# One decode layer with cached attention and an MLP: ten idle matrix products taken out ahead of the sixth group's values, and the second MLP product split four to ten between a partial sum and the result

## The chip, the cores and the metric

The kernel runs on one core of a Trainium2 chip. The core has a matrix engine (TensorE, "PE" in the profile, with its weight loads as "PEld"), a vector engine (VectorE, "DVE"), a scalar engine (ScalarE, "ACT"), a general engine (GpSimd, "POOL"), and a queue engine (SyncE, "SP") which here only issues transfers from the device's memory (DMA). The metric is the device time of one execution in microseconds, the median of several runs.

## The reference

Four tokens (batch 4, one position each, width 448) pass through an attention block over the last 1024 cached positions and then through an MLP; both add to the running sum `h`.

```python
def _A_ref(x, k_cache, v_cache, wq, wo):          # 16 query heads, 8 key/value heads, head width 256
    W = 1024                                      # only the last 1024 of 4096 cached positions
    q = (x @ wq).reshape(B, Sq, 16, 256).transpose(0, 2, 1, 3)
    k = repeat(k_cache[:, :, Sk - W:, :], 2, axis=1)
    v = repeat(v_cache[:, :, Sk - W:, :], 2, axis=1)
    p = softmax(einsum("bhqd,bhkd->bhqk", q, k) * 256 ** -0.5)
    return einsum("bhqk,bhkd->bhqd", p, v).transpose(0, 2, 1, 3).reshape(B, Sq, 4096) @ wo

def _B_ref(x, w1, b1, w2, b2):                    # 448 -> 1792 -> 448
    return gelu(layernorm(x) @ w1 + b1) @ w2 + b2

h = x + _A_ref(layernorm(x), k_cache, v_cache, wq, wo)
return h + _B_ref(layernorm(h), w1, b1, w2, b2)
```

Everything is float32. The data that has to be read is about 88 MB: two caches of 8 x 4 MB each (as far as they are used), and the four weight matrices.

## The kernel before

**Stages.** A "group" `g` is one of the eight key/value heads with its two query heads, for all four tokens. For each group the kernel projects the queries (`project_q`), forms scores against 1024 keys (`scores_half` twice, 512 keys each), takes the softmax (`softmax`), transposes the probabilities (`transpose_p`, tiles `ppt` to `pT`), multiplies them with the cached values (`values`, tile `po`), transposes and scales the result (`transposed_output`, tiles `o`, `pot`, `oT`) and multiplies it with its slice of the output weights (`add_output`, into `acc`). The groups overlap: while one is in its values, the next is in its scores. After the last group come two layer norms and the MLP: the first product `pu` (line 416), the Gelu (line 430), transposes into `gT` (lines 435 to 442), and the second product (lines 445 to 463) into `py`, to which line 465 adds the rest; line 466 writes it out.

**Columns of the matrix engine.** With only four tokens a product uses few of the engine's 128 columns. So the kernel places four products at a time at rows 0, 32, 64 and 96 of the output, one for each token, or one for each chunk of the contraction, or one for each quarter of the output's columns.

**The second MLP product.** The contraction over 1792 runs in 14 chunks `c` of 128. There are two ways to do a chunk:

- *Through a partial sum*: one product per chunk over all 448 output columns (line 449), placed at quadrant `c % 4` of a tile `pa`. All chunks of a quadrant add up there. ScalarE then copies `pa` to `pas` (line 453), and four products with a selection matrix (`add_quadrants`, line 255) add the four quadrants up into `py`.
- *Straight into the result*: four products per chunk, one for each quarter of the output columns (128, or 64 for the last of a chunk), each at its own quadrant of `py` (line 459). Nothing has to be added up behind it.

Before, eight chunks go the first way and six the second; `add_quadrants` stands behind the second of these six, so that they run while ScalarE copies.

**Idle products.** `keep_warm(n, tile)` issues `n` products of a zero tile (bf16, 32 columns of weights, 512 columns of data) into a scratch tile; nobody reads them. They stand at places where the matrix engine would otherwise sit idle. Line 340 issues ten of them between the transposes of group 7's probabilities (line 339) and the values of group 6 (line 342).

**What sets the order.** The order on the matrix engine is the program's own order, since that engine is scheduled by hand. Transfers are all issued by SP, in program order, into three large slots (`ring`). The last three slots, `te`, hold: the keys of group 7 (`k7`, 4096 KB); the values and output weights of group 6 (`vo[0]`, 4992 KB, in one transfer); the values of group 7 in three pieces (1024, 2048 and 1024 KB); its output weights (896 KB); the first MLP weights in two pieces (`w1`, 1792 and 1344 KB: contraction chunks 0 and 1, then 2 and 3); and the second MLP weights in three pieces (`w2`, 1792, 896 and 448 KB: chunks 0 to 7, then 8 to 11, then 12 and 13). Each product waits for the piece that it reads. The SP rows for the last slots, with what each issue waits for, are these (`DMAHW0` to `DMAHW7` are eight completion counters of transfers, taken in turn; `DMA te_815<-w` are the pieces of `w2`):

```order
L57 DMA te_813<-k 128x8192 [waits DMAHW5_49,PE_49]
L57 DMA te_814<-vo 128x9984 [waits DMAHW6_49,PE_49]
L57 DMA te_815<-vo 128x2048 [waits DMAHW7_49,PE_49]
L57 DMA te_815<-vo 128x4096
...
L57 DMA te_814<-vo 128x1792
L57 DMA te_813<-w 128x3584
L57 DMA te_813<-w 128x2688
L57 DMA te_815<-w 128x3584 [waits DMAHW0_49]
L57 DMA te_815<-w 128x1792 [waits DMAHW1_49]
L57 DMA te_815<-w 128x896 [waits DMAHW2_49]
```

The counters go round: `k7` has number 0, `vo[0]` number 1, the first piece of group 7's values number 2, and so on up to the first MLP weights with 6 and 7; the three pieces of `w2` have 0, 1 and 2 again. So the second piece of `w2` is issued when `vo[0]` has landed, and the third when the first piece of group 7's values has. (A row for a second piece of 2048 columns between those of 4096 and 1792 reads like the one above it and is left out.)

Of the kernel before, what the change touches and what calls it, by code (L numbers as in the profile page):

```python
# [35 lines left out]
def block_kernel(ctx: ExitStack, tc, rows, wq0, k0, wq1, la, lb, lc, ld, k7, vo, w1, w2, out):  # L36
# [165 lines left out]
    def transpose_p(g, p):  # L202
        for h in range(2):
            pt = ps_t.tile([P, 4, P], F32, tag="t", name=f"ppt{g}_{h}")
            for c in range(4):
                nc.tensor.transpose(pt[:, c, :], p[:, (4 * h + c) * P : (4 * h + c + 1) * P], ident)  # L206

            src = pt.rearrange("p (c i) (b q) -> p c i b q", i=2, b=B)
            for i in range(2):
                nc.vector.tensor_copy(  # L210
                    pT[g % 2][:, 2 * h : 2 * h + 2, :, i * REP : (i + 1) * REP], src[:, :, i, :, :REP]
                )
# [14 lines left out]
    def columns(t, j):  # L227
        if j < 3:
            return t[:, j * P : (j + 1) * P].rearrange("p (i c) -> p i c", i=2)
        return t[:, None, 3 * P :].to_broadcast([t.shape[0], 2, H])  # L230
# [22 lines left out]
    def add_quadrants(dst, t, start):  # L253
        for j in range(4):
            nc.tensor.matmul(dst[j * Q : (j + 1) * Q], sel, columns(t, j), start=start, stop=False)

    def po_tile(g, pool=ps_o, tag="o"):
        return pool.tile([P, 2, DH], F32, tag=tag, name=f"po{g}")
# [73 lines left out]
    warm0 = ps_o.tile([P, 512], F32, tag="o", name="warm0")  # L332

    def keep_warm(n, warm):
        for _ in range(n):
            nc.tensor.matmul(warm[:Q], idle[:, :Q], idle, start=True, stop=True)  # L336

    keep_warm(2, warm0)
    transpose_p(g + 1, p)
    keep_warm(10, warm0)  # L340
    po = po_tile(g)
    values(g, vt, po)
    po_last = po_tile(g + 1, ps_t, "t")
# [98 lines left out]
        nc.scalar.copy(gT[rows, 12:, :B], put[rows, 3].rearrange("p (j i) q -> p j i q", i=2)[:, :, i, :])  # L442
    keep_warm(1, warm)

    first = 8
    pa = ps_w.tile([P, D], F32, tag="acc", name="pa")
    for c in range(first):
        j, m = c % 4, Q if c < 4 else B
# [6 lines left out]
    for c in range(first, NFC):  # L455
        for j in range(4):
            m, n = (Q, 2) if c == first else (B, 2 if j < 3 else 1)
            w = columns(w2t[c], j) if n == 2 else w2t[c][:, None, 3 * P :]
            nc.tensor.matmul(
                py[j * Q : j * Q + m, :n, :], gT[:, c, :m], w, start=(c == first), stop=(c == NFC - 1),  # L460
            )
        if c == first + 1:
            add_quadrants(py, pas, False)
    res = once.tile([P, P], F32, tag="res", name="res")
    nc.vector.tensor_add(res, py.rearrange("p i c -> p (i c)"), hb)
# [72 lines left out]
```

## Time and profile before

| | us |
|---|---|
| median of three runs | 214.65 (214.59 to 214.75) |
| the profiled execution, its own time | 214.81 |
| span in its trace, first to last instruction | 213.0 |
| PE busy | 137.4 (64% of the span) |
| DVE busy | 38.4 (18%) |
| ACT busy | 21.2 (10%) |
| bytes read from the device's memory | 88.26 MB, 415 GB/s over the span |

The table reads as follows: the matrix engine has the most work of all engines, but a third of the span it does nothing. The transfers, which are not an engine's instructions, move 415 GB/s on average over the whole span. Where the one and where the other decides has to be read from the stages, which the prediction does.

### The profile page before, as it was taken

What the parts mean: (1) busy time and instruction counts of PE and PEld (TensorE: products, weight loads), DVE (VectorE), ACT (ScalarE), POOL (GpSimd) and SP (SyncE); (2) the same over time, 40 slices, a digit from 0 to 9 for tenths busy, and PEclk for the clock granted to TensorE, in tenths of its full rate; (3) what the DMA queues carried; (4) which work ended last, traced back from release to release, by engine and by line L of the source; (5) the groups of instructions that cost most, each with busy time, mean ns of one, the idle gap of its engine ahead of it and who ended that gap; (6) DMA issues with size and microseconds to landing.
All of it is one profiled execution on the core that took longest, in us unless ns stands there. A gap on an engine that the chain in (4) does not pass through costs nothing.

```text
span 213.0 us, 2294 instructions
## 1 busy us (share of the span) xinstructions
PE 137.4 (64%) x971; PEld 48.2 (23%) x971; DVE 38.4 (18%) x167; ACT 21.2 (10%) x52; POOL 5.6 (3%) x17
## 2 busy tenths in 40 slices
PE   0456824872970595289398198239809876998993
PEld 0322211220220221023123022113202322334432
DVE  1420320320230012012114013100301223122320
ACT  0210110120020100021003001000000302000310
POOL 6100000000000000000000000000000000000110
PEclk9999995796697579769859959955965999999999
DMA  7999899999999999999999999999999998999990
GB/s 291 433 392 502 381 486 391 447 467 409 417 453 444 417 417 477 390 465 391 458 423 444 425 456 417 429 417 465 405 410 415 430 450 380 435 414 435 420 376 34
DMA packets 3289, 88.46 MB, mean 415 GB/s; under 512 B 384, under 2 KB 512, under 8 KB 1104
## 3 DMA queue, kind: packets, MB, share of 16 engines
q1 hardware_dynamic: 3248, 88.29, 96.7%
q8 instruction: 7, 0.11, 0.2%
q10 hardware_dynamic: 32, 0.05, 0.1%
q14 instruction: 2, 0.02, 0.0%
HBM read 88.26 MB, written 0.07 MB: 415 GB/s over the span
## 4 chain that ended last, share of the span: by engine, by line
DMA 64%; PE 29%; DVE 3%; ACT 1%; issue 1%; SPq 0%; ACTq 0%; DVEq 0%
DMA ta<-la 21%; DMA td<-ld 20%; DMA tb<-lb 16%; PE s L174 8%; DMA t<-k 8%; PE po L218 8%; PE ppt L206 2%; PE pu L416 2%; PE warm L336 1%; PE acc L247 1%; PE pq L154 1%; PE pot L239 1%; PE pa L449 1%; DVE o L235 1%; DVE mx L179 1%
## 5 line engine op out<-in xcount | busy, mean ns | idle before, releaser
L179 DVE TENSOR_REDUCE mx<-s 128x1 f32<-128x512 f32 x16 | 11.1, 691 | 61.0 <-PE s L174 61.0
L174 PE MATMUL s<-ta,qT 128*32 128x512 f32 x64 | 12.2, 935 | 8.9 <-DMA ta<-la 8.9
L156 ACT COPY qs<-pq 128x512 f32<-128x512 f32 x8 | 4.7, 585 | 112.3 <-PE pq L154 112.3
L190 ACT ACTIVATE p<-s,nm 128x512 f32<-128x512 f32 x16 | 10.9, 687 | 45.9 <-DVE nm L186 45.9
L174 PE MATMUL s<-td,qT 128*32 128x512 f32 x32 | 7.3, 1061 | 12.0 <-DMA td<-ld 12.0
L235 DVE TENSOR_SCALAR o<-po,rec 128x512 f32<-128x512 f32 x8 | 6.0, 751 | 47.1 <-PE po L218 47.1
L218 PE MATMUL po<-tb,pT 128*32 128x512 f32 x32 | 7.3, 1061 | 10.4 <-DMA tb<-lb 10.4
L154 PE MATMUL pq<-tc,yT 128*32 128x512 f32 (+1 forms) x20 | 3.9, 890 | 14.8 <-DMA tc<-lc 14.8
L206 PE MATMUL ppt<-ident,p 128*128 128x128 f32 x64 | 10.5, 286 | 2.0 <-ACT p L190 1.7
L218 PE MATMUL po<-tc,pT 128*32 128x512 f32 x64 | 10.5, 815 | 0.0
L160 PE MATMUL pqt<-ident,qs 128*128 128x128 f32 x32 | 6.6, 341 | 6.0 <-ACT qs L156 6.0
L174 PE MATMUL s<-tb,qT 128*32 128x512 f32 x64 | 9.1, 717 | 0.0
L206 PEld LDWEIGHTS ppt<-ident,p 128*128 128x128 f32 x64 | 6.7, 140 | 7.1 <-ACT p L190 7.1
L218 PE MATMUL po<-te,pT 128*32 128x512 f32 x64 | 7.9, 596 | 0.1
L162 DVE TENSOR_REDUCE sm<-pqt 128x16 f32<-128x64 f32 x8 | 1.8, 224 | 33.9 <-PE pqt L160 33.9
L174 PE MATMUL s<-t,qT 128*32 128x512 f32 x32 | 6.1, 925 | 2.6 <-DMA t<-k 2.6
L218 PE MATMUL po<-td,pT 128*32 128x512 f32 x64 | 7.3, 595 | 0.0
L336 PE MATMUL warm<-idle 128*32 128x512 bf16 x25 | 7.3, 382 | 0.0
L160 PEld LDWEIGHTS pqt<-ident,qs 128*128 128x128 f32 x32 | 4.2, 169 | 12.1 <-ACT qs L156 10.3
L174 PEld LDWEIGHTS s<-ta,qT 128*32 128x32 f32 x64 | 2.9, 163 | 17.4 <-issue 14.4
L239 PE MATMUL pot<-ident,o 128*128 128x128 f32 x32 | 5.2, 287 | 2.2 <-DVE o L235 2.2
L148 POOL TENSOR_TENSOR r<-ve_r,mhalf 128x1 f32<-128x1 f32 x2 | 1.1, 542 | 192.2 <-DVE ve_r L147 192.2
(129 smaller groups left out, 113.4 us busy)
## 6 DMA issues: line engine op xcount, KB each, us to landing
tc<-lc SPq DMA_DIRECT2D x2, 7936.0 KB
td<-ld SPq DMA_DIRECT2D x2, 7936.0 KB
ta<-la SPq DMA_DIRECT2D x2, 7040.0 KB, 29.4
tb<-lb SPq DMA_DIRECT2D x2, 7040.0 KB, 34.3
te<-vo SPq DMA_DIRECT2D x1, 4992.0 KB, 27.2
t<-k SPq DMA_DIRECT2D x1, 4864.0 KB, 16.4
te<-k SPq DMA_DIRECT2D x1, 4096.0 KB, 36.9
te<-w SPq DMA_DIRECT2D x2, 1792.0 KB, 28.0
```

The costliest lines, as they stand in the source:

```text
L154: nc.tensor.matmul(pq[j * Q : (j + 1) * Q, cols], y, w, start=True, stop=True)
L156: nc.scalar.copy(qs, pq)
L160: nc.tensor.transpose(pt[:, i, :], qs[:, i * P : (i + 1) * P], ident)
L174: nc.tensor.matmul(s[b * Q : (b + 1) * Q, :], qT[g % 2][:, c, b, :], kt[:, c, b, :], start=(c == 0), stop=(c == 1),)
L179: nc.vector.reduce_max(m, s, axis=AX.X)
L190: nc.scalar.activation(p[:, h * 512 : (h + 1) * 512], halves[h], AF.Exp, bias=nm, scale=SCALE, accum_out=sums[:, h : h + 1],)
L206: nc.tensor.transpose(pt[:, c, :], p[:, (4 * h + c) * P : (4 * h + c + 1) * P], ident)
L218: nc.tensor.matmul(po[b * Q : (b + 1) * Q], pT[g % 2][:, c, b, :], vt[c][:, :, b, :], start=(c == 0), stop=(c == NKC // 2 - 1),)
L235: nc.vector.tensor_scalar_mul(o, po, rec)
L239: nc.tensor.transpose(pt[:, i, c], o[:, i, c * P : (c + 1) * P], ident)
L336: nc.tensor.matmul(warm[:Q], idle[:, :Q], idle, start=True, stop=True)
L416: nc.tensor.matmul(pu[j * Q : j * Q + m, :], zT[rows, a, :m], w, start=(a == 0), stop=(a == ND - 1),)
```

## The change

The ten idle products of line 340 are taken out, and the second MLP product is divided otherwise: four chunks go through the partial sum and ten straight into the result. `add_quadrants` now stands behind chunk 7, the fourth of the straight ones.

```diff
     keep_warm(2, warm0)
     transpose_p(g + 1, p)
-    keep_warm(10, warm0)
     po = po_tile(g)
     values(g, vt, po)
...
-    first = 8
+    first = 4
     pa = ps_w.tile([P, D], F32, tag="acc", name="pa")
     for c in range(first):
         j, m = c % 4, Q if c < 4 else B
...
-        if c == first + 1:
+        if c == 7:
             add_quadrants(py, pas, False)
```

On the matrix engine, behind the transposes of group 7's probabilities (`ppt`; `te_814` holds group 6's values, `warm_859` is the scratch tile), there stood before, with nine more pairs like the one shown:

```order
L206 MATMUL ppt_1_869<-ident,p_852 128x128 [waits Activation_49]
L206 MATMUL ppt_1_869<-ident,p_852 128x128 x3
L336 LDWEIGHTS idle
L336 MATMUL warm_859<-idle 32x512
...
L218 MATMUL po_886<-te_814,pT_113 32x512 [waits DMAHW1_49,PE_49]
L218 MATMUL po_886<-te_814,pT_113 32x512 x15
```

and now:

```order
L206 MATMUL ppt_1_869<-ident,p_852 128x128 [waits Activation_49]
L206 MATMUL ppt_1_869<-ident,p_852 128x128 x3
L218 MATMUL po_876<-te_814,pT_113 32x512 [waits DMAHW1_49,PE_49]
L218 MATMUL po_876<-te_814,pT_113 32x512 x15
L218 MATMUL po_893<-te_815,pT_114 32x512 [waits DMAHW2_49,DVE_49,PE_49]
```

The values of group 6 follow the transposes directly; they still wait for `vo[0]`, counter 1.

At the end of the matrix engine's program, in the second MLP product (`te_815` holds `w2`), there stood before:

```order
L449 MATMUL pa<-te_815,gT 32x448 [waits DMAHW0_49,DVE_49,Pool_49]
L449 MATMUL pa<-te_815,gT 32x448 x3
L449 MATMUL pa<-te_815,gT 4x448 x4
L459 MATMUL py<-te_815,gT 32x128 [waits DMAHW1_49]
L459 MATMUL py<-te_815,gT 32x128 x3
L459 MATMUL py<-te_815,gT 4x128 x3
L459 MATMUL py<-te_815,gT 4x64
L255 MATMUL py<-pas,sel 32x128 [waits Activation_49]
L255 MATMUL py<-pas,sel 32x128 x3
```

and now:

```order
L448 MATMUL pa<-te_815,gT 32x448 [waits DMAHW0_49,DVE_49,Pool_49]
L448 MATMUL pa<-te_815,gT 32x448 x3
L458 MATMUL py<-te_815,gT 32x128 x4
L458 MATMUL py<-te_815,gT 4x128 x3
L458 MATMUL py<-te_815,gT 4x64
...
L255 MATMUL py<-pas,sel 32x128 [waits Activation_49]
L255 MATMUL py<-pas,sel 32x128 x3
L458 MATMUL py<-te_815,gT 4x128 [waits DMAHW1_49]
```

Four full-width products and their weights are gone, sixteen narrow ones are new, and the wait for the second piece of `w2` (counter 1) has moved from ahead of `add_quadrants` to behind it. On the other engines the same instructions stand in the same order as before.

## The prediction

> **What bounds the kernel now.** I read the page's slices first (who is busy when), then the chain of waits in order of time (what the end hangs on), then the issues with their times to landing (how far the transfers are behind that chain), and last short windows at the end. Page first:
>
> ```profile
> DMA  7999899999999999999999999999999998999990
> ```
>
> The transfer engines are full in every slice but the last. In the chain up to 160 us nearly every piece is a transfer, and from there on an engine:
>
> ```profile
> 117.86 42.28 DMA td<-ld
> 180.99 0.66 PE ppt L206 x4
> 181.65 2.27 PE warm L336 x10
> 183.97 4.50 PE po L218 x40
> ...
> 208.12 0.54 ACT pas L453
> 209.12 0.92 PE py L459 x11
> 210.07 0.29 DVE res L465
> ```
>
> So the last 50 us hang on the matrix engine and its partners, and 2.27 us of that are the ten idle products, waiting for nobody. But the transfers run almost as long, so a faster chain may run into them. When does each piece of the last slots land?
>
> ```profile
> te<-vo SPq DMA_DIRECT2D x1, 4992.0 KB, 27.2
> te<-w SPq DMA_DIRECT2D x2, 1792.0 KB, 28.0
> te<-vo SPq DMA_DIRECT2D x2, 1024.0 KB
> te<-vo SPq DMA_DIRECT2D x1, 2048.0 KB
> te<-w SPq DMA_DIRECT2D x1, 1344.0 KB
> te<-vo SPq DMA_DIRECT2D x1, 896.0 KB
> te<-w SPq DMA_DIRECT2D x1, 896.0 KB, 26.1
> te<-w SPq DMA_DIRECT2D x1, 448.0 KB
> ...
> 154.46 0.33 SPq L57 DMA_DIRECT2D te<-vo  x1
> 177.61 0.44 SPq L57 DMA_DIRECT2D te<-w  x1
> 181.71 0.33 SPq L57 DMA_DIRECT2D te<-w  x1
> 184.19 0.33 SPq L57 DMA_DIRECT2D te<-w  x1
> ```
>
> `vo[0]` lands at 154.46 + 27.2 = 181.66. The first piece of w2, issued at 177.61, lands at 205.61 (two transfers share that row; were the 28.0 that of w1's first piece, issued a little ahead, the 4032 KB of three pieces would have to land in the 3 us up to 207.81). The second, issued at 181.71, lands at 207.81. The third is issued at 184.19 by a queue that waited for the first piece of group 7's values, so that one landed at 184.17. Between 184.17 and 205.61 the six pieces from 2048 KB to the 1792 of w2 come in: 8896 KB in 21.44 us, 414.9 KB per us. Taken in order of issue, they land, as an estimate from these rows, at 189.11 (2048 KB of group 7's values), 191.57 (its last 1024), 193.73 (output weights), 198.05 (w1, first), 201.29 (w1, second) and 205.61. The third of w2 is the end of the stream:
>
> ```profile
> 208.00:208.25 0.25, 0.25 (x17) 0.18 (x8) 0.00 (x0) 0.14 (x1) 0.00 (x0) 1.00 0.44 172
> 208.25:208.50 0.25, 0.22 (x9) 0.00 (x0) 0.00 (x0) 0.25 (x1) 0.00 (x0) 1.00 0.01 0
> ```
>
> (the last two columns are the transfers' share and GB/s): about 208.27. None of these issues waits for anything that the change moves, so the landings stay where they are.
>
> **The change part by part.** *The ten idle products.* Without them the values of group 6 start when the transposes are through at 181.65 and `vo[0]` is there at 181.66: at 181.70 in place of 183.97, a shift of 2.27. That is the most this edit can give; behind it, each product that waits for a piece cuts it (the first two rows are group 6's transposes and output product, used further below):
>
> ```profile
> 188.48 0.66 PE L239 MATMUL pot<-ident,o 128*128 128x128 f32 x4
> 189.61 0.96 PE L247 MATMUL acc<-te,oT 128*32 128x448 f32 x8 [0.47 <-DVE oT L243]
> ...
> 190.39 0.63 PE L218 MATMUL po<-te,pT 128*32 128x512 f32 x3
> 192.13 0.67 PE L255 MATMUL last<-accs,sel 128*32 128x128 f32 x7
> 192.54 0.63 PE L218 MATMUL po<-te,pT 128*32 128x512 f32 x3
> 195.80 1.08 PE L363 MATMUL last<-te,oT 128*32 128x128 f32 x32 [0.15 <-DVE oT L243]
> 199.57 0.96 PE L416 MATMUL pu<-te,zT 128*32 128x448 f32 x8
> 201.95 1.80 PE L416 MATMUL pu<-te,zT 128*4 128x448 f32 x16
> ```
>
> - Group 7's middle values began at 190.39. Shifted by 2.27 they would begin at 188.12, but their piece lands at 189.11. They start at 189.13: 1.26 is left, 1.0 us has become a wait. What is queued behind them on the matrix engine (the quadrant sums at 192.13, the last values, all that follows) waits along.
> - Its last values began at 192.54, would begin at 191.26, and their piece lands at 191.57: 191.60, and 0.94 is left.
> - The output weights (used 195.80 - 0.94 = 194.86, landed 193.73) and w1's first piece (199.57 - 0.94 = 198.63, landed 198.05) are there in time.
> - The third chunk of `pu` at 201.95 would come at 201.01; w1's second piece lands at 201.29, so 201.32, and 0.63 is left.
> - The second MLP product at 206.29 comes at 205.66; its first piece lands at 205.61, just in time.
>
> Gelu, transposes and copies between these are the same instructions behind the same releasers and move along.
>
> *The second MLP product.* Its rows:
>
> ```profile
> 206.29 1.71 PE L449 MATMUL pa<-te,gT 128*32 128x448 f32 x16
> 207.83 0.64 PE L459 MATMUL py<-te,gT 128*32 128x128 f32 x16
> 208.70 0.43 PE L255 MATMUL py<-pas,sel 128*32 128x128 f32 x8 [0.23 <-ACT pas L453]
> 208.94 1.05 PE L459 MATMUL py<-te,gT 128*4 128x128 f32 x32
> ...
> 207.83 0.35 PEld L459 LDWEIGHTS py<-te,gT 128*32 128x32 f32 x16 [0.65 <-DMA te<-w]
> 208.83 0.86 PEld L459 LDWEIGHTS py<-te,gT 128*4 128x4 f32 x32
> ```
>
> (Each float32 product is two records.) Eight chunks through `pa` take 206.29 to 207.83, 0.19 each. A straight chunk takes 0.86 / 4 = 0.22 by the pace of the weight loads, and behind the last one 0.22 to its end: 208.94 + 0.88 + 0.22 = 210.04, where the chain has it. The quadrant sums take 208.94 - 208.70 = 0.24. Before, the engine ran out of straight chunks at about 208.27 and waited until 208.70 for ScalarE's copy, which ends 0.66 behind `pa`'s last product (208.04). So four chunks moved cost 4 x (0.22 - 0.19) = 0.12 more and save that wait of 0.43. Without any transfers in the way: 206.29 + 0.77 (four `pa` chunks) + 0.88 (four straight) + 0.24 + 1.32 + 0.22 (six straight and the end) = 209.72, a gain of 0.32. The copy costs nothing as long as the four straight chunks cover it: `pa` is done 0.21 behind its last start, and 0.66 later the sums could start; the chunks take 0.88, so the two come out even within 0.01. Were that cover gone, the wait of 0.66 would stand there in full.
>
> With the transfers: start at 205.66; `pa` chunks to 206.43; straight chunks 4 to 7, whose weights are in the first piece, to 207.31; sums to 207.55. Chunk 8 needs the second piece, landed at 207.81: start 207.83, and 0.28 of gain has gone into this wait. (At 207.83 the old kernel met the same landing: the weight load there names it.) Six chunks and the end: 207.83 + 1.54 = 209.37; the third piece, landed at 208.27, is needed only at 208.7.
>
> **Sum**: 210.04 - 209.37 = 0.67 us off the span, 213.0 to 212.3. The profiled execution's own time goes from 214.81 to 214.14. The median of the runs is 0.16 below that execution, so 214.65 - 0.67 = 213.98.
>
> Bounds of what the trace doesn't show: whether a product that has to wait for a landing starts 0.02 behind it (the weight load at 207.83 behind 207.81) or as much as the 0.4 by which a weight load otherwise runs ahead of its products; at the end this costs 0 to 0.4, and I take the first, since it is the same landing. The straight chunks could go at 0.20 (eight records of the row of 1.05 without its last 0.25) up to 0.32 each (0.64 for two at 207.83): six of them 1.2 to 1.9 in place of 1.32, from -0.1 to +0.6; I take the middle because most of the moved ones are of the 4-column shape of the 0.86 row.
>
> **The rivals.**
>
> *The transfers don't hold it up* (the pieces come sooner than I take them, or out of turn). Then the full 2.27 + 0.32 = 2.59 comes off: 212.1. Against it: the stream's end at 208.27 and two straight chunks behind it (0.66) cannot end before 208.93, which is 1.1 off; so even a half-way case is 213.5.
>
> *The gain stays within what a measurement can tell*, which is about 0.2% or 0.43 us. The chunk price at its upper bound (0.32) gives 207.83 + 1.92 + 0.22 = 209.97, 0.07 off: 214.6. A second piece later by 0.3 gives 0.37 off: 214.3. For it: the transfer engines run out unevenly at the end, so a landing may wander; against it: the 0.86 row, and 1.54 us of work only behind the landing.
>
> *The clock falls in the new wait, and the kernel is slower.* The granted clock fell to half in the trace whenever a stretch held too little work, and not only when the engine was wholly idle:
>
> ```profile
> 26.03:29.44 3.41, 1.97 (x12) 1.25 (x12) 1.17 (x9) 1.50 (x5) 0.00 (x0) 1.00 1.07 462
> 101.11:104.53 3.42, 1.61 (x12) 0.58 (x12) 0.94 (x3) 0.00 (x0) 0.00 (x0) 1.00 1.06 449
> 152.31:155.72 3.41, 1.57 (x16) 0.53 (x12) 0.94 (x3) 0.00 (x0) 0.00 (x0) 1.00 1.03 447
> 179.61:183.02 3.41, 2.69 (x15) 1.53 (x16) 0.69 (x6) 1.33 (x4) 0.00 (x0) 1.00 0.92 386
> ```
>
> (matrix engine's busy time in the third column). The clock halved at the end of the second and the third stretch, with 1.61 and 1.57 busy, and not behind the first, with 1.97. The new low point is the wait up to 189.13: in the 3.41 us ahead of it stand 0.48 of values (group 7's first end at 183.97 + 4.50 - 2.27 = 186.20), 0.66 of transposes, 0.96 of output product and, as an estimate from ten in 2.27, 0.4 of the two idle products behind it, 2.5 in all. That is above 1.97, so it should hold. If it doesn't, one stretch of 3.41 us at half speed loses 1.71, more than the 1.26 left there: 0.45 behind the old chain, less 0.32 at the end, 0.1 slower. It decides for slower only when the following stretch stays at half speed too: at most 1.7 more, and less where the engine waits for others anyhow; with 1.5, 216.3. The ten products removed were work of this kind, but the values of group 6 take their place at once, so the stretch from 179.61 holds 1.33 of transposes and 1.32 of values, as much as before.
>
> On this the Trainium skill (TensorE: Matmul & The Clock Gate, Part 4) says that transposes don't count as work for the clock. The stretch from 179.61 agrees as little as it disagrees: 2.69 with the transposes, 1.36 without, and the clock held, while the two that fell had 0.95 and less without, as each holds one group of four transposes (0.66). By that rule the new wait's stretch has 1.84, still above 1.36: it makes the rival a little likelier, and leaves the sum as it is.
>
> **How the numbers follow.** The forecast has 0.74; the transfers not in the way (some or all) 0.05; within the measurement 0.13; the clock 0.08. So 213.98 is the time of the likeliest case; its own range is 213.7 (0.97 off, were the last wait not there) to 214.2. Over all cases the range is 213.4 (the nearer part of the first rival: 0.94 left and 0.32 from the second edit) to 214.6 (the upper chunk price). Faster by over 0.2%: 0.78, since the first rival is also faster and 0.01 of the forecast is not; within: 0.14; slower: 0.08.
>
> **What would show it.** In the changed kernel's chain a transfer should stand again in the last 30 us: `te<-vo` ahead of group 7's middle values at about 189.1, `te<-w` ahead of chunk 8 at about 207.8. The values of group 6 should start at 181.7, the second MLP product at 205.6 to 205.7, the result's addition at 209.4. The quadrant sums should start without a gap. The granted clock should read 1.00 from 166 us on. Wrong would be: the transfers end elsewhere than at 208.3; the sums wait for the copy; a straight chunk takes over 0.3; or the clock shows a half behind 181.

## The result, and the profile after

| | before | changed |
|---|---|---|
| median, 14 runs each | 214.84 us (214.59 to 216.23) | 215.13 us (214.36 to 215.68) |
| ratio, with its 95% interval | | 0.9989 (0.9973 to 1.0004) |
| profiled execution: own time, span | 214.81, 213.0 | 215.03, 213.1 |

No change that can be told from none; forecast was 213.98, with 0.14 for this outcome. The measured median lies above the stated range, which ended at 214.6.

The page after shows the first difference in its row of the granted clock (40 slices, tenths of full speed; one slice is 5.3 us):

```profile
PEclk9999996797698579769859959955967998599999
```

The last twelve digits before were "965999999999", here they are "967998599999". The clock came back earlier behind 160 us, and then it fell a second time, in the two slices from 176 to 186. Now the chain of waits in order of time (start, length, what), where before stood the ten idle products and values of 4.50:

```profile
154.75 27.07 DMA te<-vo
181.82 0.14 issue
181.95 6.92 PE po L218 x40
...
206.70 0.96 PE pa L448 x8
207.66 0.87 PE py L458 x23
208.53 0.26 PE py L255 x8
208.78 1.35 PE py L458 x21
210.16 0.29 DVE res L464
```

The values of group 6 start at 181.95, as forecast (181.70, the transfer landed 0.16 later than in the trace before). But they take 6.92 in place of 4.50, and with that the whole gain of the first edit is gone. The second product begins at 206.70 where 205.66 was forecast, and takes 206.70 to 210.13, 3.43 us, which is the sum of the forecast 0.77 + 0.88 + 0.24 + 1.54 (the chain puts the overlap of neighbouring products elsewhere, so its first and last piece read 0.96 and 1.35).

Why 6.92? The matrix engine's timeline of the changed kernel (in brackets the idle time ahead and what ended it), and behind it three stretches of 3.41 us, cut where the clock changes (columns as before: PE busy, then PEld, DVE, ACT, POOL, granted clock, transfers' share, GB/s):

```profile
176.93 0.59 PE L336 MATMUL warm<-idle 128*32 128x512 bf16 x2
179.20 1.65 PE L206 MATMUL ppt<-ident,p 128*128 128x128 f32 x8 [1.68 <-ACT p L190]
181.95 6.92 PE L218 MATMUL po<-te,pT 128*32 128x512 f32 x40 [1.10 <-DMA te<-vo]
...
176.67:180.08 3.41, 1.72 (x14) 0.73 (x8) 1.19 (x6) 1.45 (x4) 0.00 (x0) 1.00 0.90 385
180.08:183.49 3.41, 2.31 (x12) 0.82 (x14) 0.52 (x5) 0.00 (x0) 0.00 (x0) 0.50 0.97 406
183.49:186.90 3.41, 3.41 (x20) 0.90 (x16) 0.00 (x0) 0.00 (x0) 0.00 (x0) 0.50 1.01 430
```

The engine idles 1.68 us while ScalarE and VectorE do group 7's softmax, and in this execution a stretch ends just behind that. It holds 1.72 us of work, less than the 1.97 with which the clock held in the trace before, and the clock halves. The next stretch has the wait of 1.10 for `vo[0]` in it, so it isn't full, and the clock comes back only behind the one after. A half behind 181 us was one of the signs that the prediction had named for being wrong.

### The profile page after: what moved, and what is told of

Its sections match the earlier page's. It is cut to its first block, busy times and chain, and to the rows that moved or that the text cites. A ratio compares the mean times of both kernels' runs of the same rounds, so it can differ in the third digit from the quotient of the medians.

```text
span 213.1 us, 2322 instructions
## 1 busy us (share of the span) xinstructions
PE 138.1 (65%) x985; PEld 48.8 (23%) x985; DVE 38.5 (18%) x167; ACT 21.2 (10%) x52; POOL 5.6 (3%) x17
## 4 chain that ended last, share of the span: by engine, by line
DMA 66%; PE 28%; DVE 3%; ACT 1%; issue 1%; DVEq 0%; ACTq 0%
DMA td<-ld 20%; DMA tc<-lc 18%; DMA ta<-la 14%; DMA te<-vo 13%; PE po L218 10%; PE s L174 5%; PE pq L154 2%; DMA t<-wq 2%; PE pu L415 2%; PE acc L247 1%; PE ppt L206 1%; PE pqt L160 1%; PE py L458 1%; PE pot L239 1%; ACT qs L156 1%
## 5 line engine op out<-in xcount | busy, mean ns | idle before, releaser
L174 PE MATMUL s<-ta,qT 128*32 128x512 f32 x64 | 12.7, 967 | 8.4 <-DMA ta<-la 8.4
L218 PE MATMUL po<-te,pT 128*32 128x512 f32 x64 | 10.3, 761 | 1.1 <-DMA te<-vo 1.1
L210 DVE COPY pT<-ppt 128x16 f32<-128x16 f32 x32 | 4.7, 171 | 7.9 <-PE ppt L206 7.9
```

What stands on the lines that cost most here:

```text
L174: nc.tensor.matmul(s[b * Q : (b + 1) * Q, :], qT[g % 2][:, c, b, :], kt[:, c, b, :], start=(c == 0), stop=(c == 1),)
L210: nc.vector.tensor_copy(pT[g % 2][:, 2 * h : 2 * h + 2, :, i * REP : (i + 1) * REP], src[:, :, i, :, :REP])
L218: nc.tensor.matmul(po[b * Q : (b + 1) * Q], pT[g % 2][:, c, b, :], vt[c][:, :, b, :], start=(c == 0), stop=(c == NKC // 2 - 1),)
```

## The experiments

Two theories were set against each other. **A**: the clock halves near 180 us in some of the executions, where the engine idles in the softmax; how the 3.41 us stretches lie against the program decides which. **B**: the clock plays no part, the last transfers hold the end. Each kernel ran 9 to 14 times in a series; every execution gave its span and mean clock, and the kernel before ran beside them on the same chip (one chip for e1 to e4, another for e5 to e11). "Long" below means a span above 213.05 for kernels without the ten idle products and above 213.45 for those with them, limits put by eye between the groups. A long span is not proof of a halving near 180 us, and a short one not of its absence: only the profiled executions show where the clock changed.

**e1: the kernel before again.**

> The kernel before, unchanged, to see how its span and mean granted clock vary between executions. Theory A (the clock halves near 180 us in some executions, where the matrix engine idles 1.68 us in group 7's softmax; the phase of the 3.41 us stretches against the program decides): the spans fall in two groups, one near 213.0 with the clock at 0.845 to 0.856, a rarer one 1 us or more longer with the clock below 0.835. Theory B (the clock plays no part; the last transfers hold both kernels): one group of spans within 0.3 us, whatever the clock.

Measured: median 215.81, spans 212.8 to 213.3 four times and 213.7 to 214.4 eight times. With those that ran beside the other kernels the kernel before has 103 spans: 54 with a mean of 213.03 and 49 long ones with a mean of 213.97. The profiled execution, one of the long ones (213.7), on the matrix engine:

```profile
177.06 0.59 PE L336 MATMUL warm<-idle 128*32 128x512 bf16 x2
179.33 1.40 PE L206 MATMUL ppt<-ident,p 128*128 128x128 f32 x8 [1.68 <-ACT p L190]
180.66 3.90 PE L336 MATMUL warm<-idle 128*32 128x512 bf16 x10
184.62 2.78 PE L218 MATMUL po<-te,pT 128*32 128x512 f32 x24
...
177.00:180.41 3.41, 1.72 (x14) 0.93 (x9) 1.39 (x7) 1.45 (x4) 0.00 (x0) 1.00 0.79 341
180.41:183.82 3.41, 3.41 (x11) 1.16 (x10) 0.32 (x3) 0.00 (x0) 0.00 (x0) 0.51 1.00 418
```

The same 1.72, the same halving at 180.4: it belongs to the kernel before as well. There the ten idle products take 3.90 in place of 2.33; they fill the next stretch, and the clock is back after one. Theory A holds in its main point; that the long group is the larger one here, and that a mean clock of 0.849 can go with a long span, wasn't expected. The three runs seen ahead of the prediction, and the profiled one, were all of the shorter group.

**e2: only the ten out.**

```diff
-    keep_warm(10, warm0)
```

> Only the ten idle products are taken out; the second MLP product is as before. Theory A: the executions whose clock stays whole have a span of about 212.5 to 212.9 (0.24 above those of the changed kernel), those whose clock halves near 180 us some 1 us more, and the halving comes in half or more of the executions. Theory B: the end is held by the last transfers, 212.9 or more in all executions, with no relation between span and clock.

Measured: median 214.56, ratio 0.9951 (0.9932 to 0.9969); spans 212.6 to 212.9 seven times, 213.8 and 214.1. Two of nine long, where half or more were expected; the sizes fit. The profiled execution was one of the long ones:

```profile
182.09 7.41 PE L218 MATMUL po<-te,pT 128*32 128x512 f32 x40 [0.95 <-DMA te<-vo]
...
177.74:181.15 3.41, 1.72 (x10) 0.84 (x8) 1.45 (x7) 1.45 (x4) 0.00 (x0) 1.00 0.87 371
181.15:184.56 3.41, 2.47 (x12) 0.68 (x16) 0.26 (x2) 0.00 (x0) 0.00 (x0) 0.51 1.04 440
```

Again 1.72 and a halving, and a second stretch that isn't full. A ratio here depends on how many long executions fell into the series: with two groups 0.9 us apart, nine runs settle little, and the interval doesn't know of that.

**e3: only the new division.**

```diff
-    first = 8
+    first = 4
-        if c == first + 1:
+        if c == 7:
```

> Only the second MLP product is divided four to ten; the ten idle products stay. Theory A: about 0.3 us less than the kernel before in executions with a whole clock (span 212.7), since the wait of 0.43 for the copy is gone and four chunks cost 0.03 each more; as rare a halving as in the kernel before. Theory B: no change, 213.0, because the second piece of the last weights lands at 207.8 in any case and the chunks behind it are more.

Measured: median 215.32, ratio 0.9999 (0.9980 to 1.0019), spans 212.7 to 213.2 six times, 213.7 to 214.2 six times. The stage itself became shorter as forecast, in the profiled, long execution:

```profile
207.42 0.96 PE L449 MATMUL pa<-te,gT 128*32 128x448 f32 x8
208.17 1.08 PE L459 MATMUL py<-te,gT 128*32 128x128 f32 x32
209.08 0.42 PE L255 MATMUL py<-pas,sel 128*32 128x128 f32 x8
209.32 1.49 PE L459 MATMUL py<-te,gT 128*4 128x128 f32 x48
```

The quadrant sums follow without a gap, and the stage takes about 3.4 where it took 3.75. In the time nothing of this is to be seen: 0.3 us is lost in a spread of 1.5, and the six shorter spans average 212.98, 0.05 below those of the kernel before.

**e4: the changed kernel with the softmax gap filled.**

```diff
-    keep_warm(2, warm0)
+    keep_warm(8, warm0)
     transpose_p(g + 1, p)
```

> The changed kernel with eight in place of two idle products ahead of the transposes of group 7's probabilities, where the matrix engine waits 1.68 us for the softmax. At 0.21 us each they should fit in. Theory A: no halving of the clock behind 166 us in the trace, spans of 212.3 to 212.6 in nearly all executions, values of group 6 at about 181.9 right behind their transfer, time about 214.1 and the spread between executions below 0.5 us. Theory B: spans as in the changed kernel, 212.5 to 213.8, since idle products bring no transfer sooner.

Measured: median 214.57, ratio 0.9966 (0.9948 to 0.9983), spans 212.6 to 212.8 eight times and one of 213.8. No halving behind 163 us in the trace. This is the run that answers the prediction step by step:

```profile
177.04 1.89 PE L336 MATMUL warm<-idle 128*32 128x512 bf16 x8
179.32 1.33 PE L206 MATMUL ppt<-ident,p 128*128 128x128 f32 x8 [0.38 <-ACT p L190]
182.00 4.50 PE L218 MATMUL po<-te,pT 128*32 128x512 f32 x40 [1.35 <-DMA te<-vo]
189.30 1.92 PE L218 MATMUL po<-te,pT 128*32 128x512 f32 x16 [0.29 <-DMA te<-vo]
191.77 1.07 PE L218 MATMUL po<-te,pT 128*32 128x512 f32 x8 [0.33 <-DMA te<-vo]
201.47 1.80 PE L415 MATMUL pu<-te,zT 128*4 128x448 f32 x16 [0.42 <-DMA te<-w]
205.86 0.96 PE L448 MATMUL pa<-te,gT 128*32 128x448 f32 x8
207.95 1.70 PE L458 MATMUL py<-te,gT 128*4 128x128 f32 x48
...
207.95 0.76 PEld L458 LDWEIGHTS py<-te,gT 128*4 128x4 f32 x32 [0.28 <-DMA te<-w]
209.03 0.32 PEld L458 LDWEIGHTS py<-te,gT 128*4 128x4 f32 x16 [0.32 <-DMA te<-w]
```

With a whole clock the chain runs into the same transfers that the prediction named, at 182.00, 189.30, 191.77, 201.47 and 207.95 (forecast 181.70, 189.13, 191.60, 201.32, 207.83). One wait more is there: chunks 12 and 13 wait for the third piece until 209.03.

```profile
208.25:208.50 0.25, 0.25 (x19) 0.24 (x14) 0.00 (x0) 0.00 (x0) 0.00 (x0) 1.00 0.08 29
208.50:208.75 0.25, 0.25 (x17) 0.20 (x6) 0.00 (x0) 0.00 (x0) 0.00 (x0) 1.00 0.00 0
```

The transfer engines had stopped before 208.5. A piece that is through with them by 208.5 is seen by its reader at 209.03.

**e5 and e10: the gap emptied, two series.**

```diff
-    keep_warm(2, warm0)
     transpose_p(g + 1, p)
```

> The changed kernel without the two idle products ahead of the transposes of group 7's probabilities, so that the matrix engine idles 2.27 us there in place of 1.68. Theory A (a stretch of 3.41 us with 1.72 us of work or less halves the clock): the halving near 180 us comes in more of the executions than in the changed kernel (8 or 9 of 14), most spans 213.1 or longer, and the trace, if it halves, shows some 1.2 us busy in the stretch. Theory B (the halving is tied to something else, such as the transfers): the same mixture as the changed kernel.

> The kernel with the emptied gap again, since its first series had 4 halved executions of 12 where more than in the changed kernel were expected. If the share of halved executions depends on how much of a stretch is idle (theory A), it is here at least that of the changed kernel beside it, 6 of 12 or more. If it is 4 or fewer again, with more in the changed kernel, the share of halved executions doesn't follow from the idle time alone, and something else in the phase of the stretches is missing from the theory.

Measured: medians 214.57 and 214.81, ratios 0.9968 (0.9948 to 0.9988) and 0.9991 (0.9969 to 1.0012). Long were 3 of 12 in each, fewer than in the changed kernel (8 of 14 in the first series, 6 of 12 in e9). (The four halved ones that the second expectation speaks of include one with a span of 213.0 and a mean clock of 0.840.) In e5's profiled execution the clock did halve at 180.15, behind a stretch with 1.31 of work:

```profile
176.74:180.15 3.41, 1.31 (x11) 0.76 (x8) 1.31 (x7) 1.45 (x4) 0.00 (x0) 1.00 0.91 392
```

So the halving comes as theory A says, but its share doesn't grow with the idle time; both expectations of the share failed. 6 of 24 against 14 of 26 may still be chance (about 1 in 20 by an exact test), and nothing here sets the phase of the stretches. That stays open. One long execution of e10 has another cause; its profile shows no halving and the last products at the same place as e4's, but the wait for the output's write reads 2.8 us where e4 and e9 have 1.2:

```profile
SPq L530 <- DMA out<-res: 2.8, 1, 2.8
```

In the last four microseconds of this trace the DMA view lists, beside the output, one load of instructions: 16 KB on queue q8, which took 1.45 us from 210.8 on. The output's packets, through within 0.4 us in the traces of e4 and e9, took from 210.9 to 212.7 here.

**e6: gap filled, ten out, old division.**

```diff
-    keep_warm(2, warm0)
+    keep_warm(8, warm0)
     transpose_p(g + 1, p)
-    keep_warm(10, warm0)
```

> Gap filled with eight idle products, the ten out, and the second MLP product divided eight to six as before. Theory A1 (with a whole clock the end is held by the third piece of the last weights, which is seen at about 209.0, 0.7 after the transfer engines stop): the same span as with the new division, 212.6 to 212.8, and the last chunks start at about 209.0 or a little later. Theory A2 (the division is worth what it was forecast, 0.24): 212.9 to 213.0.

Measured: median 214.52, ratio 0.9963 (0.9946 to 0.9981), all twelve spans 212.5 to 212.8, mean 212.68. The same as with the new division (212.69 for the eight of e4). In its trace chunk 8 waits for the second piece, and the last four chunks take a little longer than their work:

```profile
207.99 0.64 PE L458 MATMUL py<-te,gT 128*32 128x128 f32 x16 [0.38 <-DMA te<-w]
208.58 1.14 PE L458 MATMUL py<-te,gT 128*4 128x64 f32 x32
```

So, as theory A1 has it, where the clock is whole and the ten are out the division is worth nothing that can be seen; e4 ran on another chip, so this is sure to about 0.1 us. That the third piece holds the end is seen in e4, where a weight load waits for it. In e6 it is not seen as directly: the wait on record is the one for the second piece, and the last four chunks take only 0.09 longer than in the kernel before (1.14 against 1.05). Theory B has a part in this: with a whole clock the last transfers do hold the end.

**e7: e4 with the last weights in four pieces.**

```diff
-    w2t = cut(load(e[2], CACHE, w2, (8 * D, 4 * D, 2 * D)), NFC * (D,))
+    w2t = cut(load(e[2], CACHE, w2, (6 * D, 4 * D, 3 * D, D)), NFC * (D,))
```

> The gap-filled kernel with the second MLP weights loaded in four pieces of 6, 4, 3 and 1 chunks in place of 8, 4 and 2, so that only one chunk stands behind the last landing. Theory A1 (the last landing holds the end): one chunk of 0.22 less behind it, span 212.4 to 212.5. Theory A2 (the end is held by the work behind the second piece): no change, or longer by the cost of one more transfer.

Measured: median 214.51, ratio 0.9958 (0.9942 to 0.9974), twelve spans of 212.3 to 212.6, mean 212.53: 0.15 below e6, about two thirds of the 0.22 that was expected. The wait has moved one piece forward:

```profile
208.43 1.05 PE L458 MATMUL py<-te,gT 128*4 128x128 f32 x32 [0.19 <-DMA te<-w]
```

Chunks 10 to 13 start at 208.43, behind the third piece, and run through without another wait. So it was the last landing that held the end, and now the one ahead of it does. The span is the shortest of the kernels tried; the median time is that of e6 (214.51 and 214.52).

**e8: the kernel before with the gap filled.**

```diff
-    keep_warm(2, warm0)
+    keep_warm(8, warm0)
     transpose_p(g + 1, p)
     keep_warm(10, warm0)
```

> The kernel before with eight in place of two idle products in the softmax gap; its ten behind the transposes stay. Theory A: the kernel before has the same halving in many executions, so filling the gap takes them away: spans of 212.7 to 213.2 only, no halving behind 166 us, median 0.5 below the kernel before. Theory B (only the removal of the ten made the halving): the mixture of the kernel before stays, 212.8 to 214.4.

Measured: median 214.57, ratio 0.9973 (0.9956 to 0.9990); twelve spans, all 212.6 to 213.0. The long half of the kernel before is gone, with the ten idle products still on the path. In the profiled execution they run at full speed, behind an early chain, and the values start at 183.04:

```profile
180.65 2.33 PE L336 MATMUL warm<-idle 128*32 128x512 bf16 x10
183.04 4.50 PE L218 MATMUL po<-te,pT 128*32 128x512 f32 x40
...
201.44 1.80 PE L416 MATMUL pu<-te,zT 128*4 128x448 f32 x16 [0.35 <-DMA te<-w]
207.89 0.64 PE L459 MATMUL py<-te,gT 128*32 128x128 f32 x16 [0.37 <-DMA te<-w]
```

The last two rows show that even so the chain runs into the same pieces of `w1` and `w2` as in e4 and e6 (201.47 and 207.95 in e4), so here the ten cost nothing. Against e6, which has them out and ran beside it, the mean span is 0.13 longer (212.81 and 212.68): that is what the first edit is worth where the clock stays whole.

So the softmax gap causes the halving, not the place of the ten. In the four kernels with the gap filled, 1 of 45 spans is above 213.05 (213.8 in e4, with a mean clock of 0.853; it wasn't profiled).

**e9: the changed kernel again.**

> The changed kernel, unchanged, beside the next two kernels on one chip. Theory A: spans in two groups again, 212.5 to 213.0 with a whole clock and 213.1 to 213.8 with a halving near 180 us, the second in about half of the executions; the kernel before beside it in two groups as well, 212.7 to 213.3 and 213.5 to 214.4. Theory B: one group.

Measured: median 215.41, ratio 1.0015 (0.9993 to 1.0038); spans 212.5 to 212.8 six times, 213.4 to 214.4 six times. The profiled one has a halving and yet a span of 212.8:

```profile
181.99 6.18 PE L218 MATMUL po<-te,pT 128*32 128x512 f32 x40 [0.56 <-DMA te<-vo]
...
178.64:182.05 3.41, 1.37 (x12) 0.93 (x16) 1.14 (x9) 1.45 (x4) 0.00 (x0) 1.00 0.78 327
182.05:185.46 3.41, 3.41 (x20) 0.98 (x24) 0.00 (x0) 0.00 (x0) 0.00 (x0) 0.50 1.04 442
```

Here the stretch ends behind the wait for `vo[0]`; the next one is full, the clock is back after 3.41 us, and the 1.68 us lost are no more than the transfers would have cost anyhow. So a halving of one stretch cost nothing here. It isn't always so: in e1 the stretch behind was full as well, and the execution was a long one.

The median of this series is high for a second reason: in four of its twelve executions the time is 2.7 to 3.0 us above the span, in the others 1.8 to 1.9.

**e11: four idle products in the gap.**

```diff
-    keep_warm(2, warm0)
+    keep_warm(4, warm0)
     transpose_p(g + 1, p)
```

> The changed kernel with four idle products in the gap in place of two: 0.43 us less idle, so that the poorest stretch holds 1.72 + 0.43 = 2.15 us of work. Theory A with a limit between 1.72 (halved) and 1.97 (held): no halving at 180 us but for stretches that also take in the wait for group 6's values; spans 212.5 to 213.0 in nearly all executions. Theory A with a limit above 2.15: the mixture of the changed kernel.

Measured: median 214.87, ratio 0.9989 (0.9970 to 1.0008), nine spans of 212.6 to 213.0 and three of 213.3. The profiled one is one of the three: it has no halving behind 166 us, its products end within 0.1 us of where e4's do, and the wait for the output's write reads 1.7 where e4 has 1.2, with a load of instructions at 210.1 as in e10. So four were enough in what was seen, and the limit lies below the 2.20 of its stretch from 179.55:

```profile
179.55:182.96 3.41, 2.20 (x17) 1.21 (x21) 0.76 (x7) 1.45 (x4) 0.00 (x0) 1.00 0.96 402
```

Whether the other two of 213.3 are of the same kind wasn't seen.

## Why the prediction was wrong

Three of its steps failed: that the clock would hold across the softmax, that the third piece of the last weights would be there at 208.27, and that the time would follow the span of one execution.

*The chain and the ten idle products.* Right: taken out, they let the values start at once behind `vo[0]`, and the shift was cut by the pieces that were named, and by one more (below). e4 has each of the five waits within 0.3 us of its forecast.

*The clock.* This step failed. "That is above 1.97, so it should hold" was said of the wait at 189, where nothing happened. The stretch that broke was the one across the softmax, of which the prediction said that it "holds 1.33 of transposes and 1.32 of values, as much as before". That was true of one way to lay the stretches, the one of the profiled execution, and they lie otherwise in every execution. Moved by 0.7 us the trace before has a stretch with hardly more work than the 1.72 that halved the clock:

```profile
176.91:180.32 3.41, 1.73 (x18) 0.33 (x7) 1.37 (x4) 0.83 (x3) 0.00 (x0) 1.00 0.83 355
```

The third rival had the mechanism, at another place. Its price, 0.1 to 1.6 us slower than the kernel before, was about right against the 213.0 of the trace before: the profiled execution is 0.1 longer, the mean of the long ones 0.5. The ten idle products were also worth something when the clock had halved: they filled the next stretch, and the clock came back after 3.41 us (e1, e3). Without them the engine waits there for `vo[0]`, and the clock stays at half for 6.8 us (the changed kernel, e2). That the cover of this wait was lost is the part that the sum left out. In the profiled execution the halving took the gain of the first edit; over all executions it does not explain the missing gain, since the kernel before has as many long ones (next paragraph).

*The time before.* The prediction took the profiled span of 213.0 for the kernel. It is that of the shorter group; over 103 executions the mean is 213.48. The changed kernel has 12 spans with a mean of 212.65 and 14 long ones with 213.56, together 213.14. Within the shorter group the span gains 0.38, within the long one 0.4, over all 0.34 (0.16%), and the share of long ones, 14 of 26 against 49 of 103, is the same within chance. So the span does gain about half of the forecast 0.67. How much of it the edits earn in an execution of like kind is less sure, since the short executions of two kernels needn't have their stretches at the same place: with the gap filled it is only 0.13 (e8 and e6). The medians, 0.9989 and 1.0015 of the kernel before, depend on how many long ones a series drew, and on the next point.

*The time behind the span.* The prediction let the time follow the span, 214.81 to 214.14. In the 103 executions of the kernel before the time is 1.74 to 1.87 us above the span; in 6 of the 26 of the changed kernel it is 2.6 to 3.0 above. So the mean time gains only 0.07 (215.26 to 215.19) where the mean span gains 0.34. Over all kernels with both edits the difference is above 2.2 in 14 of 83 executions, in the others in none of 148. None of the 14 was profiled, so the cause stays open. The traces give a hint: five of the eight with the new division (e3, e4, e7, e10, e11) have one more load of 16 KB of instructions, behind 209 us, in e4 even behind the end of the span; the five traces with the old division have none there.

*The third piece of the last weights.* A term was missing: "the third piece, landed at 208.27, is needed only at 208.7" took the stop of the transfer engines for the landing. It is seen at 209.03, and two chunks behind it end at 209.70 in place of 209.37. That is 0.33 of the forecast 0.67, put at nothing in its sum. The trace before has a sign of the lag: the second piece landed at 207.81, and the 448 KB behind it, 1.1 us at the pace of 414.9 KB per us, were through 0.5 us later.

*The second MLP product.* The price of the chunks was right (3.43 forecast and measured). What it was to bring, 0.32 less a wait of 0.28 in the sum, and 0.24 against the old division in the expectation of e6, isn't seen: with the last landing in the way the spans are the same (e4 and e6), and alone it doesn't show (e3).

*Transposes and the clock.* The prediction left open whether transposes count as work for the clock. Two stretches answer it: one of the trace before, of which the transposes of `ppt` and `pqt` make up the whole 1.97, and one of e10, with `ppt` for 1.31 of 2.02. These are the rows of those tiles alone in them, `ppt` and `pqt` of the kernel before, then `ppt` of e10 (columns: PE, PEld, DVE, clock, transfers):

```profile
26.03:29.44 3.41, 1.31 (x8) 0.84 (x8) 0.58 (x4) 1.00 1.07 462
26.03:29.44 3.41, 0.66 (x4) 0.42 (x4) 0.22 (x1) 1.00 1.07 462
```

```profile
179.35:182.76 3.41, 1.31 (x8) 0.84 (x8) 0.58 (x4) 1.00 0.93 390
```

The clock held behind both, with 0 and 0.71 of other work, while 0.95 of other work beside 0.66 of transposes was not enough at 104.53. (At 179.27, where the clock changes of e10 put it, its stretch has 1.95 in all.) So they count here, against what the Trainium skill says (TensorE: Matmul & The Clock Gate, Part 4), whose measured example is a bf16 transpose; these are float32. The sum of all products sorts the stretches nearly without exception. Cut every 3.41 us from the first clock change on, the thirteen traces have 467 stretches at full clock: the 110 with 1.72 us of products or less all halved it, the 351 with more than 1.82 all held it, and the six in between went either way. Without the transposes there is no such limit: a stretch with none at all held it (26.03), while one with 1.09 of other products, 1.68 with its transposes, halved it (e11, from 152.3).

## What to carry to other kernels

Where a stage shows a gap of the matrix engine of half a clock stretch, lay the stretch over it at every phase, not at the one that the profiled execution happened to have; fill the gap where the engine waits anyhow, not behind it, where filling costs time. Before a forecast of less than one per cent, look at the distribution of the kernel's spans: when it has two groups, ask what divides them first, since that is worth more than the change. And a transfer's last byte isn't its landing: take the time at which a reader of an earlier piece was released. Last, compare the time with the span in every execution: a gain in the span can be lost behind it.

## What the runs showed of the hardware

- In all thirteen traces the clock changes lie whole multiples of 3.41 us apart, at another place against the program in each. A stretch with 1.72 us of products or less halved the clock, one with more than 1.82 held it. To come back it took about 2.7 us in a stretch at half clock: of 252 such stretches all 109 with 2.72 or more brought it back, and of the 143 with 2.69 or less only one did (2.66, in the changed kernel).
- Idle products that fit into a wait cost nothing and saved 0.67 us of mean span in the kernel before (213.48 to 212.81, e8).
- The queue engine's wait for the output's write read 1.2 us in nine traces, and 1.3, 1.4, 1.7 and 2.8 in e7, e3, e11 and e10. These four are the ones in which a load of 16 KB of instructions ran between 209.4 us and the end of the span.
